# Where attention loads and w_out look-ahead stand in the bursts of a fused attention and two-MoE kernel

## The chip, the cores and the metric

The kernel runs on one core of one Trainium2 chip. The metric is device time in microseconds (us), the median of three runs. The engines are TensorE (PE), VectorE (DVE), ScalarE (ACT), GpSimd (POOL) and SyncE (SP). SP computes nothing here: it issues nearly all loads, in program order.

## What is computed

Attention in chunks of 64 tokens over 8 batches, 8 heads and 576 tokens, its output as 4608 rows of 512, and two gated products after it:

```python
attn = softmax(q_c @ k_c.T / 8)            # per chunk of 64, head dim 64
x = (attn @ v_c)                           # as 4608 x 512
x = ((x @ w_a) * (x @ w_b)) @ w_out        # 512 -> 1536 -> 512
h = ((x @ w1) * (x @ w2)) @ w3             # 512 -> 1024 -> 1024
out = h @ w_out2                           # 1024 -> 512
```

## The kernel before

The 4608 rows are nine blocks of 512. Phase 0 is the first gated product, phase 1 the second (w3 and its w_out are multiplied together once). In phase 0 the first pair of blocks is done by `plain_step`: 24 steps, in each the two products of one of 12 columns of 128 features, split in high and low parts (three matmuls for each product). The block written second lags by three steps (`order`, `AHEAD`). The next three pairs are done by `block_steps`, with a Strassen scheme of seven products (`strassen_step`); the ninth block stands alone.

Each pair leaves the second block's gated values in G tiles. They are multiplied with w_out only afterwards, in `burst`: 12 steps of 12 matmuls each in phase 0, one w_out tile of 128x1024 (512 KB) to a step. After its first step the burst also does the 12 matmuls that the pair before left pending. In parallel a list of pieces ("others") is worked off at one point per step, up to the eighth: DVE and ACT form the Strassen parts xP of the next pair. From the fifth step on the burst also advances attention for the pair after that. Phase 0 has four such bursts; below, the first stands ahead of the second pair, the second ahead of the third, the third ahead of the fourth pair.

Three queues of loads meet on SP in a burst:

- w_out tiles (`wo_f`), looked ahead by `Outs.ahead(n)`: it loads the next n tiles of the order into four homes. A home can be overwritten only when PE is done with the tile in it, so such a load can wait for PE, and all that follows on SP waits with it.
- attention loads (q and k of a unit as `qk`, v as `v`). A unit is one head pair of one block. They are put in a list by `ask` and issued one by one: `tick(loads=1)` at each of the four parts of a burst step, `tick(loads=3)` at each Strassen product; `settle(unit.qk_end)` issues all that are still due when a unit's `turn` is written. Units of the pair after the first use 32-wide rows, 16 transfers of 32 KB for q and k and ten for v.
- for the second pair only, parts of w_a and w_b: `first_sums[n].load()` (`su`, 512 KB) and `load_part` (`w_f_i`, 512 KB, or 256 KB for i = 3).

What moves on SP is thus set by where each call stands in the program and by the waits ahead of it; no planner is between. SP's transfers use eight semaphores in turn, so a transfer is issued only when the eighth before it has landed.

A `Track` emits its pieces in proportion to points that have passed, out of a number of points that is given to it. For the plain steps' attention that number was `4 * (len(order) - n) - 2`, here 82; steps with T = 1 call `point` three times and the others five, which makes 81 calls.

Of the kernel before, what the change touches and what calls it, by code (L numbers as in the profile page):

```python
# [78 lines left out]
def chunk_attention_two_gated_products(  # L79
# [59 lines left out]
    asks = {"left": deque(), "all": 0, "done": 0}  # L139
# [6 lines left out]
    def settle(n):  # L146
        while asks["done"] < n and asks["left"]:
            nc.sync.dma_start(*asks["left"].popleft())  # L148
            asks["done"] += 1

    def tick(every=False, loads=0):
        settle(asks["done"] + loads)
        for s in stores:
            s[0] += 1
        while stores and (every or stores[0][0] > 1):
            _, queue, to, src = stores.popleft()
            queue.dma_start(to, src)  # L157
# [92 lines left out]
    state = {"banks": ("rB", "rD")}  # L250
# [388 lines left out]
    def w_tile(n, name):  # L639
        return pool.tile([P, 2, 2, 2, P], F32R, tag=f"w{n}", name=name)  # L640

    def whole(t):
        return t.rearrange("p o s k n -> p (o s k n)")
# [94 lines left out]
    def load_part(ph, f, i):  # L738
        t = w_tile(4 * (f % 2) + i, f"w{ph}_{f}_{i}")
        if i < 3:  # L740
            nc.sync.dma_start(whole(t).bitcast(F32), dw[ph][f][0 if i == 0 else i + 1])
        else:
            nc.sync.dma_start(
                t[:, 0].rearrange("p s k n -> p (s k n)").bitcast(F32), dw[ph][f][1][:, NT:]
            )
        pairs.setdefault((ph, f), {})[i] = t
# [263 lines left out]
    def ready(ph, j, f, gplaces):  # L1010
        return g_parts(gplaces[f // 4][:, f % 4], f"{ph}_{j}b{f}", nc.gpsimd)

    def back(order):
        last = order[::-1]
        return [last[1], last[0], *last[2:]]

    def burst(ph, j, order, gplaces, others, at, first=None):

        n = NF[ph]
        order = back(order)  # L1020
        sums = []
        state["banks"] = ("acc2", "acc3")
        track = Track(others, 2 * n // 3)
        parts = [ready(ph, j, order[0], gplaces) if first is None else first]
        parts.append(ready(ph, j, order[1], gplaces))
        state["outs"].ahead(3)
        for f in range(n):
            if f and f + 2 < n:
                parts.append(ready(ph, j, order[f + 2], gplaces))
            s = Second(ph, j, f, state["outs"].next(), parts[f], sums, ("rC", "rA", "rB", "rD"))  # L1030
            s.part()
            s.part()
            track.point()
            if f > 3:
                for a in at:
                    a.point()
            s.rest()
            if f == 0:
                state["pending"].rest()
                parts.append(ready(ph, j, order[2], gplaces))  # L1040
            state["outs"].ahead(3)
        track.finish()
        state["pending"], state["banks"] = None_(), ("rB", "rD")

# [81 lines left out]
    with tc.manual_schedule():  # L1126
# [72 lines left out]
        order = plain_order(0, AHEAD)  # L1199
# [23 lines left out]
        units = unit_list(1)  # L1223
        both = attention_pieces(U[NHP:] + units)
        cut = 1 + 8 * NHP
        late = Track(both[:cut], 5 * AHEAD)
        at = None
        for n, (T, f) in enumerate(order):
            if T == 0:
                conv = Track([conv_piece()] * (1 if f == 0 else 3), 5 if f + 1 < AHEAD else 8)  # L1230
                if f + 1 == NF[0]:
                    conv = None
            if T == 1 and f == 0:
                late.finish()
                at = Track(both[cut:], 4 * (len(order) - n) - 2)

            def point(pe=True):
                if conv:
                    conv.point(pe)
                (at or late).point(pe)  # L1240

            if n + 1 == len(order):
                state["ready"] = ready(0, 1, NF[0] - 2, plain[0])
            plain_step(0, 0, T, f, f"0_{T}_{f}", point, plain[0], sums[0], "AC")
            if conv and (T == 1 or f + 1 < AHEAD):
                conv.finish()
                pump.flush()
# [106 lines left out]
        first_sums = {}  # L1354
        up = [list(range(n)) for n in NF]
        orders = {(0, 0): up[0]}
# [15 lines left out]
        for ph, sb in [(0, sb) for sb in range(1, NSB + 1)] + [(1, sb) for sb in range(NSB + 1)]:  # L1372
            lone = ph == 0 and sb == NSB
            begins = ph == 1 and sb == 0
            if begins:
                state["outs"] = Outs(1, wanted[1])
            state["outs"].ahead(2)
            if lone:
                x, pieces = lone_pieces(x32, f"{ph}{sb}")
                pieces = pieces + o2_pieces()  # L1380
                pump.cap = len(pump.jobs)
                pump.homes(["xo1", "xo2"], ["G2"])
                pieces += [(0.1, False, lambda: pump.load())] * 3
            elif not begins:
                x, pieces = strassen_pieces(x32, f"{ph}{sb}", sb == NSB)
            if ph == 0 and sb == 1:
                for n_ in range(2):
                    first_sums[n_] = summed(ph, orders[ph, sb][n_], n_)
                    first_sums[n_].load()
                for n_, i in ((0, 0), (0, 3), (1, 0)):  # L1390
                    load_part(ph, orders[ph, sb][n_], i)
                pieces = pieces + first_sums[0].pieces()
            steps, at, conv = NF[ph], [], []
            if ph == 0 and not lone:
                units = unit_list(sb + 1)
                attention_begins(units)
                if sb == 1:
                    settle(units[0].qk_end)
                    load_part(ph, orders[ph, sb][1], 3)
                work = attention_pieces(units)  # L1400
                n_pts = PTS * steps + steps - 4
                if sb == NSB - 1:
                    pump.cap += 3 * NF[1]
                    pump.homes(["Y0", "Y1"], ["Y2"])
                    for _ in range(3):
                        pump.load()
                    conv = later_conv(3 * NF[1])
                    work = merged((0, 1, work), (0, 1, conv))
                    n_pts = PTS * steps
                at.append(Track(work, n_pts - 3))  # L1410
            if not begins:
                done = (ph, sb - 1) if sb else (ph, 0)
                burst(ph, j + 1, orders[done], places, pieces, [] if conv else at, state.pop("ready", None))
            if lone:
                got = []
                for n_ in range(4):
                    load_w3(n_)
                at.append(Track(between(got), 5 * steps - 15))
                xs = {}

                def next_x():
                    diffs = deque()
                    for i in range(2):
                        t = pool.tile([P, 4, NT], F32, tag=f"G{i}", name=f"xd{i}")
                        diffs.extend(t[:, n_] for n_ in range(4))
                    xs["x"], xs["pieces"] = strassen_pieces(got, "10", diffs=diffs)

                early = [(0.1, False, lambda: (at[0].finish(), next_x()))]
                early += [(0.7, False, lambda n_=n_: xs["pieces"][n_][2]()) for n_ in range(18)]
                late = Track(early, 11)  # L1430
                class After:
                    n = 0

                    def point(self, pe=True):
                        self.n += 1
                        if self.n > 5 * steps - 15:
                            late.point(pe)

                    def finish(self):
                        late.finish()  # L1440

                at.append(After())
                lone_steps(ph, x, at)
                for p in xs["pieces"][18:]:
                    p[2]()
                x32, x = got, xs["x"]
                continue
            if ph == 1 and sb < NSB:
                got = []
                js = [LONE] if sb == NSB - 1 else [2 * sb + 2, 2 * sb + 3]  # L1450
                at.append(Track(x2_pieces(js, got), PTS * steps - 3))
            j, places = block_steps(ph, sb, x, at)
            if ph == 0:
                x32 = [u.x32 for u in units]
            elif sb < NSB:
                x32 = got
# [47 lines left out]
```

## Time and profile before

| | |
|---|---|
| median of three runs | 1638.82 us (1638.47 to 1640.89) |
| profiled execution | 1642.08 us, its span 1640.3 us |
| PE busy | 1559.8 us, 95% of the span |
| PEld / DVE / ACT / POOL busy | 76% / 52% / 34% / 30% |
| PE's share of the chain that ended last | 78% |
| DMA | 356.31 MB, mean 217 GB/s |

PE is busy almost throughout, so the time is PE's work plus the stretches in which PE waits or runs at a lower clock. Busy shares of the other engines say little; what matters is what ended each of PE's waits, and how SP's issues stand to it in time.

### The profile page before, as it was taken

How to read it: one execution, taken by the hardware profiler on the slowest of the kernel's cores; microseconds unless marked ns; L12 is line 12 of the kernel's file. 1: busy time of each engine (PE TensorE's matmuls, PEld its weight loads, DVE VectorE, ACT ScalarE, POOL GpSimd, SP SyncE). 2: the span in 40 equal slices, each digit the busy share in tenths (PEclk: the TensorE clock that was granted, in tenths of full speed). 3: DMA queues.
4: the chain of work that ended last, by engine and by line, in shares of the span. 5: the costliest groups of instructions: out<-in, count | busy, mean ns of one | idle time of the engine just before them, and what ended most of it. 6: DMA issues, size and time to landing. Idle time of an engine off the chain costs nothing.

```text
span 1640.3 us, 24184 instructions
## 1 busy us (share of the span) xinstructions
PE 1559.8 (95%) x8968; PEld 1254.6 (76%) x8968; DVE 858.3 (52%) x1384; ACT 551.4 (34%) x989; POOL 490.5 (30%) x502
## 2 busy tenths in 40 slices
PE   4889997899998999999999899999999999999998
PEld 3668776677777777787777677888878878878887
DVE  5667756486756555476775235545542442442331
ACT  5545444222343222433234223333421321321322
POOL 1223333222243211442225112223521421421422
PEclk8899998999999999999999999999999999999999
DMA  9977844787726787379984799776366266266184
GB/s 223 291 224 248 273 154 129 227 249 229 251 85 188 202 225 228 106 223 335 343 281 164 270 313 322 307 268 247 118 223 217 75 221 221 71 216 205 67 292 155
DMA packets 277013, 356.31 MB, mean 217 GB/s; under 512 B 174240, under 2 KB 194720, under 8 KB 276896
## 3 DMA queue, kind: packets, MB, share of 16 engines
q1 hardware_dynamic: 249728, 265.63, 52.9%
q0 software_dynamic: 23616, 81.80, 13.0%
q10 hardware_dynamic: 3552, 7.34, 1.3%
q8 instruction: 71, 1.16, 0.3%
q14 instruction: 46, 0.38, 0.1%
HBM read 268.70 MB, written 85.98 MB: 216 GB/s over the span
## 4 chain that ended last, share of the span: by engine, by line
PE 78%; DVE 6%; DMA 5%; issue 3%; ACT 3%; SPq 3%; POOL 1%; DVEq 0%; POOLq 0%; ACTq 0%
PE P L857 40%; PE acc L886 21%; PE pa L843 4%; PE pb L843 4%; PE wf L1115 3%; DMA wo<-dwo 3%; SPq L148 2%; PE pb0L L843 2%; PE pa0L L843 2%; PE x L407 1%; PE s L356 1%; DVE c L945 1%; DMA qk<-in_q_dram 1%; ACT xP L253 1%; PE t L478 1%
## 5 line engine op out<-in xcount | busy, mean ns | idle before, releaser
L857 PE MATMUL P<-xP,w 128*128 128x512 f32 (+1 forms) x3066 | 704.5, 382 | 11.6 <-DVE c L945 8.6
L857 PEld LDWEIGHTS P<-xP,w 128*128 128x128 f32 x3066 | 550.4, 188 | 135.2 <-DVE c L945 13.4
L945 DVE TENSOR_TENSOR c<-P,c 128x512 f32<-128x512 f32 (+1 forms) x228 | 150.4, 662 | 332.6 <-PE P L857 331.9
L942 ACT COPY c<-P 128x512 f32<-128x512 f32 (+1 forms) x228 | 128.4, 564 | 227.4 <-PE P L857 227.1
L973 POOL TENSOR_TENSOR G<-c,c 128x512 f32<-128x512 f32 x68 | 89.7, 1319 | 332.5 <-DVE c L945 332.4
L253 ACT CAST gh<-c 128x512 fp32r<-128x512 f32 x68 | 42.2, 621 | 329.6 <-DVE c L972 329.6
L254 POOL TENSOR_TENSOR gl<-c,gh 128x512 fp32r<-128x512 f32 x68 | 90.7, 1334 | 171.7 <-ACT gh L253 171.7
L886 PE MATMUL acc<-gh,wo 128*128 128x512 f32 x384 | 138.0, 397 | 0.0
L972 DVE TENSOR_TENSOR c<-P,c 128x512 f32<-128x512 f32 x68 | 47.0, 692 | 135.1 <-PE P L857 135.0
L886 PE MATMUL acc<-wo,gh 128*128 128x512 f32 x320 | 111.1, 390 | 0.5 <-ACT gh L253 0.5
L157 POOL DMA_DIRECT2D dw<-w x58 | 32.3, 558 | 176.5 <-DVE w L254 80.2
L886 PEld LDWEIGHTS acc<-gh,wo 128*128 128x128 f32 x384 | 72.5, 189 | 15.8
L254 DVE TENSOR_TENSOR xP<-xP,xP 128x512 fp32r<-128x512 f32 (+1 forms) x56 | 65.1, 1203 | 28.1 <-ACT xP L253 28.1
L843 PE MATMUL pa<-xq,w 128*128 128x512 f32 x288 | 76.0, 416 | 0.0
L886 PE MATMUL acc<-gl,wo 128*128 128x512 f32 x192 | 75.3, 392 | 0.0
L843 PE MATMUL pb<-xq,w 128*128 128x512 f32 x288 | 71.1, 396 | 0.0
L886 PEld LDWEIGHTS acc<-wo,gh 128*128 128x128 f32 x320 | 60.1, 188 | 13.4 <-ACT gh L253 1.0
L895 ACT COPY ev<-acc 128x512 f32<-128x512 f32 x72 | 42.4, 588 | 80.0 <-PE acc L886 75.1
L843 PEld LDWEIGHTS pa<-xq,w 128*128 128x128 f32 x288 | 57.0, 201 | 13.2 <-ACT xq L253 0.3
L886 PE MATMUL acc<-wo,gl 128*128 128x512 f32 x160 | 62.7, 392 | 0.8 <-POOL gl L254 0.8
L843 PEld LDWEIGHTS pb<-xq,w 128*128 128x128 f32 x288 | 52.9, 188 | 10.8
L373 ACT ACTIVATE e<-e 128x512 f32<-128x512 f32 x36 | 22.8, 632 | 90.5 <-DVE e L367 90.5
(158 smaller groups left out, 2369.8 us busy)
## 6 DMA issues: line engine op xcount, KB each, us to landing
w<-dw SPq DMA_DIRECT2D x175, 512.0 KB, 4.6
wo<-dwo SPq DMA_DIRECT2D x128, 512.0 KB, 4.5
dw<-w POOLq DMA_DIRECT2D x58, 512.0 KB, 4.2
w<-dw SPq DMA_DIRECT2D x75, 256.0 KB, 3.8
su<-d SPq DMA_DIRECT2D x20, 512.0 KB, 5.1
x2d<-ev POOLq DMA_DIRECT2D x36, 256.0 KB, 3.7
x<-x2d SPq DMA_DIRECT2D x36, 256.0 KB, 4.7
out_dram<-ev POOLq DMA_DIRECT2D x36, 256.0 KB, 3.0
```

Of the source, the lines that this page charges most:

```text
L148: nc.sync.dma_start(*asks["left"].popleft())
L253: nc.scalar.copy(dst_h, src)
L254: eng_l.tensor_tensor(dst_l, src, dst_h, op=ALU.subtract)
L843: nc.tensor.matmul(ps, w[m][:, kk // 2, wp, kk % 2], xq[kk // 2][:, kk % 2, xp], start=(n == 0), stop=(n == 3 * KM - 1),)
L857: nc.tensor.matmul(ps, w[:, wp, kt], x[:, kt, xp], start=(begins and n == 0), stop=(n == 5), skip_group_check=True,)
L886: nc.tensor.matmul(acc[m], a, b, start=(f == 0 and (wp, gp) == SEQ[0]), stop=(f == NF[ph] - 1 and (wp, gp) == SEQ[-1]),)
L895: nc.scalar.copy(t, acc[m])
L942: nc.scalar.copy(t, src)
L945: add = lambda o, a, b: nc.vector.tensor_tensor(o, a, b, op=ALU.add)
L972: nc.vector.tensor_tensor(g, last, c11, op=ALU.mult)
L973: nc.gpsimd.tensor_tensor(g_place(ph, nm.split("_")[0], f, gplaces), c22, c12, op=ALU.mult)
L1115: nc.tensor.matmul(ps, t[:, gp, jj], wo2[jj // 2][:, jj % 2, wp], start=(jj == 0 and (wp, gp) == SEQ[0]), stop=(jj == NF[1] - 1 and (wp, g ...
```

## The change

- In a burst, `state["hold"]` is set ahead of the first step and cleared after it. While it is set, `tick` issues no attention loads.
- After the first step `Outs.ahead` looks four tiles ahead in place of three, so the fifth tile's load is written one step earlier.
- For the second pair, two `su` loads and four `load_part` calls are no longer written ahead of the burst; they become six pieces among the others. The settling of the first unit's q and k ahead of the burst is gone.
- The number of points of the plain steps' attention track becomes the number of calls less three: 78 in place of 82.

```diff
     def tick(every=False, loads=0):
-        settle(asks["done"] + loads)
+        settle(asks["done"] + (0 if state.get("hold") else loads))
...
         track = Track(others, 2 * n // 3)
+        state["hold"] = True
...
             if f == 0:
                 state["pending"].rest()
                 parts.append(ready(ph, j, order[2], gplaces))
-            state["outs"].ahead(3)
+                state["hold"] = False
+            state["outs"].ahead(3 if f else 4)
...
-                at = Track(both[cut:], 4 * (len(order) - n) - 2)
+                at = Track(both[cut:], sum(3 if T_ else 5 for T_, _ in order[n:]) - 3)
...
             if ph == 0 and sb == 1:
+                begins_with = []
                 for n_ in range(2):
                     first_sums[n_] = summed(ph, orders[ph, sb][n_], n_)
-                    first_sums[n_].load()
-                for n_, i in ((0, 0), (0, 3), (1, 0)):
-                    load_part(ph, orders[ph, sb][n_], i)
+                    begins_with.append((0.1, False, first_sums[n_].load))
+                for n_, i in ((0, 0), (0, 3), (1, 0), (1, 3)):
+                    begins_with.append(
+                        (0.1, False, lambda f=orders[ph, sb][n_], i=i: load_part(ph, f, i))
+                    )
+                for n_, p in enumerate(begins_with):
+                    pieces.insert(4 + 3 * n_, p)
                 pieces = pieces + first_sums[0].pieces()
...
-                if sb == 1:
-                    settle(units[0].qk_end)
-                    load_part(ph, orders[ph, sb][1], 3)
```

On SP at the first burst, before: the six loads for the second pair and the first unit's q, k and v stand ahead of the burst's first w_out load, `wo_7` (the fifth tile that the burst uses).

```order
L763 DMA su_11_2887<-d_0_11_155 128x1024
L763 DMA su_10_2889<-d_0_10_154 128x1024
L741 DMA w_11_0_2891<-dw_11_0_108 128x1024
L743 DMA w_11_3_2893<-dw_11_1_109 128x512
L741 DMA w_10_0_2895<-dw_10_0_104 128x1024
L148 DMA qk_0_2897<-in_q_dram 32x8x32 x8
L148 DMA qk_0_2897<-in_k_dram 32x8x32 x8
L743 DMA w_10_3_2917<-dw_10_1_105 128x512
L148 DMA v_0_2898<-in_v_dram 64x2x64 x2
...
L148 DMA qk_1_2899<-in_q_dram 32x8x32 x2
L726 DMA wo_7_3011<-dwo_7_171 128x1024
```

On SP at the first burst, now, from the first w_out load on:

```order
L726 DMA wo_7_2947<-dwo_7_171 128x1024
L148 DMA qk_0_2887<-in_q_dram 32x8x32 x2
L763 DMA su_11_2961<-d_0_11_155 128x1024
L763 DMA su_10_2968<-d_0_10_154 128x1024
L148 DMA qk_0_2887<-in_q_dram 32x8x32 x4
L741 DMA w_11_0_2995<-dw_11_0_108 128x1024
L148 DMA qk_0_2887<-in_q_dram 32x8x32 x2
L726 DMA wo_6_3010<-dwo_6_170 128x1024
L148 DMA qk_0_2887<-in_k_dram 32x8x32 x2
L743 DMA w_11_3_3024<-dw_11_1_109 128x512
```

`wo_7` has moved ahead of all of them, and the six loads and the attention loads now stand between it and the later w_out tiles.

On SP at the end of the first burst, before, around `wo_0`, the tile of the burst's last step:

```order
L148 DMA v_1_2900<-in_v_dram 64x2x64 x4
L726 DMA wo_1_3220<-dwo_1_165 128x1024
L148 DMA qk_2_3125<-in_q_dram 32x8x32 x4
L726 DMA wo_0_3246<-dwo_0_164 128x1024
L148 DMA qk_2_3125<-in_q_dram 32x8x32 x4
```

And now:

```order
L148 DMA qk_1_2889<-in_q_dram 32x8x32 x4
L726 DMA wo_1_3198<-dwo_1_165 128x1024
L148 DMA qk_1_2889<-in_q_dram 32x8x32 x4
L148 DMA qk_1_2889<-in_k_dram 32x8x32 x8
L148 DMA v_1_2890<-in_v_dram 64x2x64 x2
L726 DMA wo_0_3234<-dwo_0_164 128x1024
```

Fourteen attention transfers stand between the last two tiles where four stood; twelve of them are settled for the second unit's `turn`.

On SP at the second burst, before (`wo_4` is again the fifth tile, `wo_11` the last):

```order
L148 DMA qk_0_4995<-in_q_dram 32x12x32 x4
L148 DMA qk_0_4995<-in_q_dram 32x4x32 x4
L148 DMA qk_0_4995<-in_k_dram 32x12x32 x4
L726 DMA wo_4_5088<-dwo_4_168 128x1024
...
L726 DMA wo_10_5288<-dwo_10_174 128x1024
L148 DMA qk_1_4997<-in_k_dram 32x12x32 x2
L148 DMA qk_1_4997<-in_k_dram 32x4x32 x4
L148 DMA v_1_4998<-in_v_dram 64x3x64 x2
L726 DMA wo_11_5318<-dwo_11_175 128x1024
```

And now:

```order
L726 DMA wo_4_5053<-dwo_4_168 128x1024
L148 DMA qk_0_4995<-in_q_dram 32x12x32 x4
L148 DMA qk_0_4995<-in_q_dram 32x4x32 x4
L726 DMA wo_5_5110<-dwo_5_169 128x1024
...
L726 DMA wo_10_5282<-dwo_10_174 128x1024
L148 DMA qk_1_4997<-in_q_dram 32x4x32 x4
L148 DMA qk_1_4997<-in_k_dram 32x12x32 x4
L148 DMA qk_1_4997<-in_k_dram 32x4x32 x4
L148 DMA v_1_4998<-in_v_dram 64x3x64 x2
L726 DMA wo_11_5318<-dwo_11_175 128x1024
```

Twelve q and k transfers moved from ahead of `wo_4` to behind it, and fourteen transfers stand ahead of `wo_11` where eight stood.

## Rows read from the trace of the kernel before

**Rows 1.** PE's waits over the span: releaser, us in total, times, longest

```profile
PE acc L886 <- DMA wo<-dwo: 15.2, 6, 7.4
```

**Rows 2.** Timeline of PE, first burst: start us, us, operation, count, [idle before, releaser]

```profile
261.57 0.50 PE L886 MATMUL acc<-gh_1b,wo 128*128 128x512 f32 x1
...
264.43 0.39 PE L886 MATMUL acc<-gh,wo 128*128 128x512 f32 x1
...
267.15 0.39 PE L886 MATMUL acc<-gh_1b,wo 128*128 128x512 f32 x1
...
283.18 0.76 PE L886 MATMUL acc<-gh_1b,wo 128*128 128x512 f32 x1 [7.40 <-DMA wo<-dwo]
...
308.35 0.51 PE L886 MATMUL acc<-gh_1b,wo 128*128 128x512 f32 x1 [2.65 <-DMA wo<-dwo]
...
312.76 7.03 PE L857 MATMUL P<-xP,w 128*128 128x512 f32 x30
```

**Rows 3.** Timeline of SP's issues in the first burst, same columns

```profile
260.28 4.71 SPq L148 DMA_DIRECT2D qk<-in_q_dram  x8
265.03 5.61 SPq L148 DMA_DIRECT2D qk<-in_k_dram  x8
...
271.18 6.45 SPq L148 DMA_DIRECT2D v<-in_v_dram  x10
...
278.92 0.34 SPq L726 DMA_DIRECT2D wo<-dwo  x1
279.31 1.91 SPq L148 DMA_DIRECT2D qk<-in_q_dram  x4
...
301.32 0.47 SPq L726 DMA_DIRECT2D wo<-dwo  x1
```

**Rows 4.** Windows: stretch, length, busy us of the engines, PEclk, DMA share, GB/s

```profile
275.00:280.00 5.00, 0.78 (x4) 0.32 (x2) 5.00 (x5) 1.36 (x3) 3.35 (x3) 0.79 0.24 47
280.00:285.00 5.00, 1.82 (x4) 1.49 (x5) 4.96 (x10) 1.22 (x2) 0.00 (x0) 0.50 0.92 248
...
470.00:480.00 10.00, 9.81 (x71) 7.76 (x70) 2.96 (x5) 1.82 (x4) 2.08 (x2) 1.00 0.01 2
...
500.00:520.00 20.00, 16.64 (x102) 13.18 (x101) 16.24 (x27) 5.04 (x9) 4.49 (x4) 1.00 0.65 168
```

**Rows 5.** Line 726's landing times, of its issues at 483.93, 508.74 and 301.32

```profile
DMA to landing us min/median/max: 3.4/3.4/3.4
...
DMA to landing us min/median/max: 4.8/4.8/4.8
...
DMA to landing us min/median/max: 6.9/6.9/6.9
```

**Rows 6.** Timeline of SP's issues ahead of and in the second burst

```profile
451.73 3.85 SPq L148 DMA_DIRECT2D qk<-in_q_dram  x8
455.63 1.97 SPq L148 DMA_DIRECT2D qk<-in_k_dram  x4
483.93 0.34 SPq L726 DMA_DIRECT2D wo<-dwo  x1
...
508.74 0.41 SPq L726 DMA_DIRECT2D wo<-dwo  x1
509.19 2.88 SPq L148 DMA_DIRECT2D qk<-in_k_dram  x6
...
514.23 0.54 SPq L726 DMA_DIRECT2D wo<-dwo  x1
```

**Rows 7.** Timeline of PE in the second burst: its two waits

```profile
503.68 0.69 PE L356 MATMUL s<-kT,qT 64*64 64x64 f32 x32 [1.81 <-DVE kT L345]
...
518.42 0.47 PE L886 MATMUL acc<-gh_3b,wo 128*128 128x512 f32 x1 [1.55 <-DMA wo<-dwo]
```

**Rows 8.** Timeline of SP in the third burst: its last six w_out issues

```profile
704.87 16.18 SPq L726 DMA_DIRECT2D wo<-dwo  x6
```

**Rows 9.** Timeline of PE, end of the plain steps

```profile
260.85 0.79 PE L407 MATMUL x<-pT,v 64*64 64x64 f32 x32 [1.01 <-ACT pT L494]
```

## The prediction

> **What bounds the kernel now.** I read the waits of PE first, since PE is busy for 95% of the span. Of what ends PE's waits, w_out tiles lead: 15.2 us in six waits [rows 1]. Two of these stand in the first burst and make up 10.05 us, 7.40 and 2.65 [rows 2]. The reader is to see there that 12 matmuls of one burst step take 2.72 us (264.43 to 267.15), and that the step behind the shorter wait, also 12 matmuls, takes 4.41 (308.35 to 312.76): 1.7 us more. The windows say why: the granted clock falls to 0.79 and then to 0.50 of full speed, that is to the lower of its two levels of 1.2 and 2.4 GHz, behind the long wait [rows 4]. So a wait costs its length and then up to another 2.7 us, if all 12 matmuls of a step take twice their 2.72.
>
> Next I read what SP did during the long wait. From 260.28 to 278.92 its track is a solid row of attention issues [rows 3], and the w_out tile that PE wants is issued only at 278.92, 4.3 us before PE goes on. While PE stood, the DMA engines were busy for 24% of 275 to 280 [rows 4]. The wait is thus one for SP's place in the queue, not for bandwidth. The numbers that I use of SP: a q or k transfer costs it 0.48 us when nothing presses (1.91 for four) and 0.65 in the busy start (16 from 260.28 to 270.64), a v transfer 0.645 (6.45 for ten), a contiguous one some 0.44 with its gap [rows 3]. A w_out tile lands 3.4 to 6.9 us after its issue [rows 5].
>
> **The change part by part. First burst.** PE would run it, never waiting, from 261.57 in a first step of 2.86, the pending 2.72, ten steps of 2.72 and 0.62 for the scores that stand inside (an estimate, the length of a 32-matmul attention group by the 0.69 in [rows 7]), and would want the last tile, `wo_0`, at about 295.0. `wo_7` can now be issued as soon as the first step is over, 264.4, and is there by 269 even at 4.8: the 7.40 us go, for that tile is wanted near 275.3. But SP still has to issue what lies between, and it starts on it only then: `wo_7` waits for PE, and all behind it waits too. From the order, between `wo_7` and `wo_0` stand 56 transfers: 32 of q and k, 12 of v, 12 contiguous ones (six for the second pair, six w_out tiles). At 0.57 for a q or k, the middle of its two prices: 32 x 0.57 = 18.2, 12 x 0.645 = 7.7, 12 x 0.44 = 5.3, `wo_7` itself 0.4. `wo_6` overwrites the tile of the third step, so it can't go before 272.6, where SP arrives at 271.0: 1.6. Sum 33.2, hence 297.9. No row shows six such loads inside a burst; they bring 2.5 MB, and each transfer waits until the eighth before it has landed. Eight issues at 0.48 take 3.8 us. Bounds: nothing, if the loads land in 3.4 us [rows 5], and 3 us, if three of the six land in 4.8 and hold SP for 1.0 each. I take 1.5, since DMA was already 92% busy in 280 to 285 with only two w_out tiles and attention in it [rows 4]. So `wo_0` goes out at 299.4 and lands, at 4.8, at 304.2. PE waits there for some 9 us, and the last step runs at the lower clock: with 4.4 to 5.4 us for it the burst ends near 309.1, against 312.76. **First burst: -3.7.** Its ends: q and k at 0.48, no hold-up, 3.4 to land, gives 304.2, or -8.6; q and k at 0.65, 3 us of hold-up and 6.9 to land gives 315.3, or +2.5.
>
> **Second burst.** Here the hold does harm. Before, the first twelve transfers of q and k were issued at 451.73 to 457.6 [rows 6], 26 us before `wo_4`, in a stretch that ends with the DMA engines nearly idle (1% of 470 to 480) [rows 4]. What hid them was the Strassen step that PE was in. Now `wo_4` stands ahead of them and waits for the burst's first step, so they are issued from 484.3 on. Eight of them fit in the gap in which SP waits for `wo_5` anyway; four more push later ones back, and by the order 14 transfers stand between `wo_10` and `wo_11` where eight stood. `wo_10` leaves at 508.74 as before, because it waits for PE. Then seven q and k by 512.6; the next must wait for `wo_10` to land, 508.74 + 4.8 = 513.5 [rows 5]; five more at 0.48 end at 516.0, two of v at 517.3. `wo_11` leaves 3.1 us after its 514.23. PE waited 1.55 for it [rows 7]; now 4.6. That lies between 2.65 and 7.40, and behind both the clock fell [rows 2], while behind 1.81 and 1.55 [rows 7] it stayed at 1.00 in 500 to 520 [rows 4]. So the last step costs another 1.7. **Second burst: +4.8.** Its ends: +1.4 (`wo_10` and `wo_11` land in 3.4, clock kept) and +6.8 (one us more of landing, 2.7 for the clock). The first unit's scores are not later for it: its last k goes out by 498 and has landed by 502, and PE got DVE's transpose only at 503.68 before, too [rows 7].
>
> The Trainium skill speaks against this part: "DMA: Bandwidth & Descriptors", section "Rules for kernel authors", says to issue a DMA early and to wait on it late, so that its fixed cost lies under compute. The rows of 451.73 to 457.6 agree, and by that rule alone the hold would only cost, here and in the first burst.
>
> **The rest.** In the third burst SP's last six w_out issues come 2.7 us apart, in the rhythm of PE's steps [rows 8]: SP waits for PE and not the other way. The hold puts twelve more transfers behind the first tile there too, some 6 us of issuing, most of which fits in such waits; the middle tiles then leave up to 0.5 us late. From the freeing of a home to the use of its next tile are two steps, 5.4 us, of which landing takes 3.4 to 4.8 [rows 5]: +0.3, with 0 and +1.5 as ends. In the fourth burst and in all four of phase 1 SP's order is word for word the same, because no attention is due and the fifth tile stands at the same place among SP's other rows: 0. The moved `su` and `w` loads are not missed where they were (they waited there for PE), and nobody needs them before the burst's last third. With 78 points in place of 82 attention's pieces in the plain steps come some 5% earlier. Its last unit's f and x still stand back to back, now one step earlier, so its 1.01 us of wait [rows 9] moves and stays; elsewhere short waits of that size may come or go: 0, with two of them (-2 and +2) as ends.
>
> **Sum:** -3.7 + 4.8 + 0.3 + 0 = +1.4. The profiled execution took 1642.08 us (span 1640.3), 3.3 more than the median; I know no reason for that to be in these bursts, so I add the sum to the median: 1638.82 + 1.4 = **1640.2**.
>
> **The rivals.** *Faster:* SP is less of a limit than I think. It issues at 0.48 all through, the six loads don't hold it up, `wo_0` is there by 299.6 (-8.6), and in the second burst the clock is kept (+1.4): -7.2, 1631.6. For it: the DMA engines had room in 275 to 280 [rows 4], and 1.91 for four [rows 3] is the price in the very burst. Against it: 16 transfers in a row took 0.65 each [rows 3], and just such runs of 16 and 12 now stand in the burst. *Slower:* in the first burst the wait for `wo_7` is exchanged for one as long for `wo_0`, since the second pair's 2.5 MB and 44 attention transfers have to pass ahead of it in a time in which PE needs only 30 us. With `wo_0` landing at 309.7 the burst ends at 315.3, +2.5, and the second burst's +4.8 stands: +7.3, 1646.1. It decides from `wo_0` landing after 306.4 on, since the burst then saves no more than 1.5. For it: the tile at 301.32 took 6.9 us to land [rows 5]. Against it: by my sum `wo_0` is issued two us before the 301.32 of before [rows 3], and other tiles landed in 3.4 to 4.8 [rows 5]. The skill's rule of the early issue leads to this case; the first burst of before speaks against it, where early issue was what made PE wait. *Without effect:* from the third burst on hardly any row of SP moves, so the change does nothing there; that is in the sum already.
>
> **How the numbers follow.** A measurement of this kernel can tell some 0.2% (3.3 us) from no change. My forecast, within 0.2%, gets 0.46; the faster rival 0.24; the slower one 0.30, more than the other because the second burst's loss rests on fewer assumptions than the first burst's gain. The likeliest's own range is 1635.5 to 1642.1. The ends of all terms together, -9.2 and +12.6, are not expected at once; the range for eight in ten runs from the faster rival to just past the slower: 1632 to 1647.
>
> **What would show it.** Right: in the first burst no wait of PE at the fifth step, a single one of 7 to 11 us at the last, SP solid from 264 to 300; in the second burst the first q and k behind 484, a wait of 4 to 5 us for `wo_11` and a slow step behind it; phase 1 as long as before. Wrong: `wo_0` there when PE wants it, so that the first burst is 10 us shorter; the second burst's clock at 1.00 throughout; or a difference that lies in the plain steps or behind the third burst.

## Result and profile after

The changed kernel takes 1649.79 us (median of five, 1647.92 to 1653.49) against 1638.82: a ratio of 1.0066, 95% interval 1.0048 to 1.0085. It is slower by 11 us, outside the range of 1632 to 1647. Its profiled execution took 1651.72 us, its span 1649.9.

To find where the time went I cut both traces at PE's first matmul of each stage and took the differences of the lengths. The third column is what the prediction had.

| stage | after less before, us | predicted |
|---|---|---|
| start, up to the first product | +0.5 | 0 |
| plain steps, up to the first burst's first matmul | +2.4 | 0 |
| first burst (51.19 to 51.07) | -0.1 | -3.7 |
| Strassen steps of the second pair | +1.6 | 0 |
| second burst (40.3 to 45.4) | +5.1 | +4.8 |
| Strassen steps of the third pair | +0.1 | 0 |
| third burst (36.0 to 38.4) | +2.4 | +0.3 |
| Strassen steps of the fourth pair | -0.2 | 0 |
| fourth burst | -2.0 | 0 |
| all that follows | -0.1 | 0 |
| sum | +9.7 | +1.4 |

The -2.0 of the fourth burst is no gain of the change: of the six kernels below that are as before from the second burst on, four are shorter there by 2.0 to 2.1 us and two longer by 0.8 to 1.0. A single profiled execution carries such chances; the difference of the medians is 11.0. The execution of before that was profiled is one of them: it took 3.3 us more than its median, and for all thirteen kernels below the stages add up to less than the difference of the medians, by 0.7 to 5.9 us. In which stage that execution was long is not settled; what p_points says of it stands there.

PE's waits after the change, over the span, in the columns of [rows 1] (waiting line, releaser: us in total, times, longest):

```profile
PE acc L886 <- DMA wo<-dwo: 18.6, 8, 6.4
```

The waits for w_out did not shrink from the 15.2 us of [rows 1]; they grew to 18.6.

**First burst.** PE's timeline after the change, to hold against [rows 2] (start us, us, operation, count, [idle before, releaser]):

```profile
264.47 0.50 PE L886 MATMUL acc<-gh_1b,wo 128*128 128x512 f32 x1 [0.85 <-DVE G0p L996]
...
282.04 0.47 PE L886 MATMUL acc<-gh_1b,wo 128*128 128x512 f32 x1 [0.65 <-DMA wo<-dwo]
...
287.15 0.47 PE L886 MATMUL acc<-gh_1b,wo 128*128 128x512 f32 x1 [2.13 <-DMA wo<-dwo]
...
310.31 0.76 PE L886 MATMUL acc<-gh_1b,wo 128*128 128x512 f32 x1 [6.37 <-DMA wo<-dwo]
...
315.54 0.64 PE L857 MATMUL P<-xP,w 128*128 128x512 f32 x2
```

The 7.40 us at the fifth step are gone, as meant. In their place stand 0.65, 2.13 and 6.37, and the last step takes 5.23 us (310.31 to 315.54) in place of 2.72. SP's timeline shows why `wo_0` is late (to hold against [rows 3]):

```profile
267.55 0.35 SPq L726 DMA_DIRECT2D wo<-dwo  x1
267.95 2.50 SPq L148 DMA_DIRECT2D qk<-in_q_dram  x2
270.61 0.87 SPq L763 DMA_DIRECT2D su<-d  x2
...
277.61 0.34 SPq L726 DMA_DIRECT2D wo<-dwo  x1
...
295.83 0.39 SPq L726 DMA_DIRECT2D wo<-dwo  x1
296.57 1.79 SPq L148 DMA_DIRECT2D qk<-in_q_dram  x4
298.40 6.44 SPq L148 DMA_DIRECT2D qk<-in_k_dram  x8
304.89 1.26 SPq L148 DMA_DIRECT2D v<-in_v_dram  x2
306.25 0.54 SPq L726 DMA_DIRECT2D wo<-dwo  x1
```

`wo_7` goes out at 267.55, one step after the burst's start, and `wo_0` at 306.25: 38.7 us for what stands between. The last 10.4 of these (295.83 to 306.25) go to 14 attention transfers, 12 of them settled at one place for the second unit's `turn`; eight k alone take 6.44. What SP waited for between the two issues (268 to 306.3), in the columns of [rows 1]:

```profile
SPq L148 <- DMA w<-dw: 1.8, 3, 1.3
SPq L726 <- DMA su<-d: 1.6, 1, 1.6
...
SPq L726 <- PE s L356: 0.6, 1, 0.6
```

With two smaller rows for w_out tiles (0.7 and 0.3) this is 4.4 us until an earlier transfer had landed, and with one more for PE (0.3) only 0.9 us for PE.

The windows (stretch, length, busy us of PE, PEld, DVE, ACT, POOL, granted clock, DMA share, GB/s), to hold against [rows 4]:

```profile
275.00:280.00 5.00, 5.00 (x24) 4.13 (x23) 5.00 (x4) 4.25 (x8) 4.48 (x4) 1.00 1.09 341
280.00:285.00 5.00, 4.35 (x19) 2.99 (x17) 5.00 (x8) 1.75 (x3) 1.39 (x2) 1.00 1.07 342
...
310.00:315.00 5.00, 4.69 (x11) 3.75 (x12) 1.86 (x4) 1.65 (x3) 1.12 (x2) 0.50 0.47 128
```

The DMA engines, 24% busy in 275 to 280 before, are now full from 275 to 285. After its wait PE runs at the lower clock (0.50) in 310 to 315.

**Second burst.** SP and then PE after the change, to hold against [rows 6] and [rows 7]:

```profile
488.30 0.32 SPq L726 DMA_DIRECT2D wo<-dwo  x1
488.71 3.94 SPq L148 DMA_DIRECT2D qk<-in_q_dram  x8
...
513.72 0.41 SPq L726 DMA_DIRECT2D wo<-dwo  x1
514.17 1.85 SPq L148 DMA_DIRECT2D qk<-in_q_dram  x4
516.07 3.91 SPq L148 DMA_DIRECT2D qk<-in_k_dram  x8
520.02 1.30 SPq L148 DMA_DIRECT2D v<-in_v_dram  x2
521.42 0.54 SPq L726 DMA_DIRECT2D wo<-dwo  x1
```

```profile
525.71 0.76 PE L886 MATMUL acc<-gh_3b,wo 128*128 128x512 f32 x1 [4.50 <-DMA wo<-dwo]
```

The first q and k are issued behind `wo_4`, at 488.71, 14 transfers stand between `wo_10` and `wo_11`, and PE waits 4.50 us. Its last step then runs at a granted clock of 0.50 (525 to 530).

**Third burst.** PE after the change; before, it never waited for w_out there:

```profile
717.39 0.47 PE L886 MATMUL acc<-gh_5b,wo 128*128 128x512 f32 x1 [1.09 <-DMA wo<-dwo]
724.01 0.47 PE L886 MATMUL acc<-gh_5b,wo 128*128 128x512 f32 x1 [0.54 <-DMA wo<-dwo]
```

**Plain steps.** PE's waits in 100 to 265, of before and then of after:

```profile
PE x L407 <- ACT pT L494: 1.6, 2, 1.0
PE f L491 <- DVE e L381: 1.3, 2, 0.6
PE s L356 <- ACT x L421: 0.5, 1, 0.5
```

```profile
PE t L478 <- issue: 3.4, 2, 1.7
PE x L407 <- ACT pT L494: 1.1, 3, 0.7
PE acc L886 <- DVE G0p L996: 0.9, 1, 0.9
```

3.4 us of waits became 5.4. Two of the new ones, 1.69 each, stand ahead of a unit's transposes on PE (L478), where "issue" names nothing that the profile shows; the 0.85 stands ahead of the burst's first matmul, which now waits for DVE's gated values.

**Strassen steps of the second pair.** The same wait of 1.82 us for DVE, in before and in after:

```profile
380.53 1.66 PE L857 MATMUL P<-xP,w 128*128 128x512 f32 x6 [1.82 <-DVE c L945]
```

```profile
383.37 2.62 PE L857 MATMUL P<-xP,w 128*128 128x512 f32 x6 [1.82 <-DVE c L945]
```

Behind it six matmuls take 1.66 us in the one and 2.62 in the other, because the granted clock fell to 0.78 in 385 to 390.

### The profile page after: what moved, and what is told of

Its sections match the earlier page's. It is cut to its first block, busy times and chain, and to the rows that moved or that the text cites. A ratio compares the mean times of both kernels' runs of the same rounds, so it can differ in the third digit from the quotient of the medians.

```text
span 1649.9 us, 24177 instructions
## 1 busy us (share of the span) xinstructions
PE 1564.0 (95%) x8968; PEld 1255.4 (76%) x8968; DVE 855.8 (52%) x1384; ACT 550.8 (33%) x989; POOL 491.2 (30%) x502
## 4 chain that ended last, share of the span: by engine, by line
PE 79%; DVE 6%; DMA 5%; issue 3%; SPq 3%; ACT 3%; POOL 1%; DVEq 0%; POOLq 0%; ACTq 0%
PE P L857 40%; PE acc L886 21%; PE pa L843 4%; PE pb L843 4%; PE wf L1117 3%; SPq L148 2%; PE pb0L L843 2%; PE pa0L L843 2%; DMA wo<-dwo 2%; PE x L407 1%; PE s L356 1%; DMA w<-dw 1%; DVE c L945 1%; DMA qk<-in_q_dram 1%; DMA qk<-in_k_dram 1%
## 5 line engine op out<-in xcount | busy, mean ns | idle before, releaser
L945 DVE TENSOR_TENSOR c<-P,c 128x512 f32<-128x512 f32 (+1 forms) x228 | 150.5, 662 | 335.1 <-PE P L857 334.4
L843 PEld LDWEIGHTS pa<-xq,w 128*128 128x128 f32 x288 | 56.3, 200 | 12.8
```

The source lines that it names most:

```text
L843: nc.tensor.matmul(ps, w[m][:, kk // 2, wp, kk % 2], xq[kk // 2][:, kk % 2, xp], start=(n == 0), stop=(n == 3 * KM - 1),)
L945: add = lambda o, a, b: nc.vector.tensor_tensor(o, a, b, op=ALU.add)
```

## Experiments

The theory after the result: in the first burst each of the two edits (the hold with its early tile, and the moved six loads) takes `wo_7`'s wait away by itself. Together they leave no attention load and no weight load ahead of the burst, so all goes through SP behind `wo_7`, and the wait comes back at the last tile. The hold costs something in the second and third burst as predicted; the points cost two of PE's waits in the plain steps. The rivals: the six loads fill the DMA engines and are alone to blame; the differences outside the bursts are chances of one execution. Each run is compared with before on its own chip, where before took 1637.6 to 1639.7.

The stages of all runs, each less before in us, and the times with their ratio to before on the same chip:

| kernel | plain | burst 1 | Strassen 2 | burst 2 | burst 3 | median us, ratio (95%) |
|---|---|---|---|---|---|---|
| p_points | +2.5 | -4.1 | +1.6 | -0.5 | -0.2 | 1642.97, 1.0035 (1.0019 to 1.0052) |
| p_hold | +1.7 | -9.6 | -0.1 | +5.1 | +1.4 | 1638.83, 1.0002 (0.9988 to 1.0017) |
| hold_only | 0.0 | -9.6 | 0.0 | +5.2 | +2.2 | 1637.68, 0.9997 (0.9985 to 1.0008) |
| p_hold_first | +1.3 | -9.6 | +1.6 | +0.7 | -0.3 | 1634.63, 0.9975 (0.9957 to 0.9994) |
| hold_first_4all | +1.3 | -8.3 | +2.4 | -0.3 | -0.2 | 1635.28, 0.9976 (0.9958 to 0.9993) |
| p_loads | +1.1 | -7.3 | +3.3 | -0.4 | -0.4 | 1636.45, 0.9988 (0.9975 to 1.0001) |
| quiet_first | -1.5 | -13.1 | +37.1 | +1.2 | +0.4 | 1661.23, 1.0142 (1.0123 to 1.0161) |
| changed kernel | +2.4 | -0.1 | +1.6 | +5.1 | +2.4 | 1649.79, 1.0066 (1.0048 to 1.0085) |
| a_no_points | -0.4 | -0.6 | +1.1 | +5.0 | +2.4 | 1649.62, 1.0061 (1.0037 to 1.0086) |
| a_first_only | +4.0 | -0.1 | +2.7 | +0.6 | -0.3 | 1645.73, 1.0039 (1.0024 to 1.0053) |
| a_loads_early | +3.7 | +0.3 | +1.2 | +5.2 | +2.9 | 1653.87, 1.0086 (1.0060 to 1.0111) |
| a_qk_early | +1.1 | -4.9 | +1.6 | +5.1 | +1.8 | 1644.66, 1.0024 (1.0005 to 1.0042) |
| a_ahead4_all | +3.8 | -7.1 | +11.1 | +3.4 | +1.9 | 1654.73, 1.0095 (1.0065 to 1.0125) |

The plain column holds about +-1.5 us of chance: kernels whose plain steps are those of before, word for word, lie between -1.5 and +1.7, since the granted clock of 40 to 140, 0.85 to 1.00, and short waits there differ from one execution to the next.

### One part of the change alone

The points alone:

```diff
-                at = Track(both[cut:], 4 * (len(order) - n) - 2)
+                at = Track(both[cut:], sum(3 if T_ else 5 for T_, _ in order[n:]) - 3)
```

> The kernel before with one edit: 78 points for the plain steps' attention in place of 82. Theory: of the 10 us lost, 2.4 lie in the plain steps and come from this edit (other neighbours of attention's transposes, and G0p waited for at the burst's start); expected +2 to +3 us, 1641 to 1642, with the first burst starting 2 to 3 us later. Rival: the 2.4 us were chance of one execution (clock, waits that the profile calls issue); expected 0, within 1 us of before.

The trace shows the waits of the changed kernel at the same places. PE's timeline:

```profile
144.31 1.06 PE L478 MATMUL t<-ident,qk 128*128 128x128 f32 x8 [1.69 <-issue]
```

All six kernels here with 78 points have two waits of 1.68 or 1.69 at L478, and none of those with 82 has them. So the points cost 2.0 us of waits. In this kernel's profiled execution the first burst gives the time back: its two waits for w_out are 7.02 and 1.46 in place of 7.40 and 2.65 [rows 2], and its last step keeps the full clock and takes 2.8 us in place of 4.4.

The median rose by 5.2 us, more than the 2 to 3 expected and than the stages, which add up to 0.0. Without the burst's -4.1 they would add up to 4.1. The burst's steps and SP's order in it are those of before; whether its 47.1 us in place of 51.2 are a chance of one execution or come with the 78 points is not shown. The column "burst 1" is held against the 51.2 of that one execution. If they were a chance of it, all entries of the column are some 4 us too low, the -0.1 of the changed kernel too; the differences among the other kernels don't rest on it.

The hold and the early fourth tile in all bursts (p_hold), and the hold with three tiles ahead everywhere (hold_only):

```diff
+        state["hold"] = True
...
+                state["hold"] = False
-            state["outs"].ahead(3)
+            state["outs"].ahead(3 if f else 4)
```

> The kernel before with the hold and the four-tile look-ahead only; the second pair's loads stay ahead of the burst. Theory (place in SP's queue): in the first burst wo_7 goes out near 271.5 and is there in time, 32 small transfers stand between it and wo_0, which lands near 298; that burst ends some 10 us earlier; the second burst loses 5 us as in the changed kernel. Sum -5, about 1634. Rival: the hold itself harms the first burst too, because loads that lay under the plain steps come late; then no gain there and +5 in all, 1644.

> The kernel before with the hold in all bursts, but three tiles ahead everywhere. Theory (the hold alone pushes the first twelve q and k behind: 14 transfers between wo_10 and wo_11 as in the changed kernel): second burst 45 to 46 us (40.3 before), a wait of 4 to 5 us for wo_11 and the lower clock behind it; third burst +1.5 to +3; first burst 42 to 45 us, a little longer than with the early fourth tile (41.6); in all 1638 to 1641. Rival (the tile that is looked ahead, for which SP waits, does it): second and third burst within 1 us of before, 1632 to 1635.

Both first bursts are 9.6 us shorter, so the early tile brings nothing; the hold alone does it. Both second bursts lose 5.1 to 5.2, by a wait for w_out of 4.28 and 4.51. PE in hold_only:

```profile
511.94 0.77 PE L886 MATMUL acc<-gh_3b,wo 128*128 128x512 f32 x1 [4.51 <-DMA wo<-dwo]
```

The rival for hold_only (the looked-ahead tile does it) falls. The times tell little: gain and losses nearly cancel, -2 to -3 by the three bursts, and the interval of hold_only runs from -2.5 to +1.3 us. The 1634 expected of p_hold was not reached.

Why the hold gains so much by itself is in p_hold's SP timeline:

```profile
261.88 4.78 SPq L148 DMA_DIRECT2D qk<-in_q_dram  x8
266.71 4.89 SPq L148 DMA_DIRECT2D qk<-in_k_dram  x8
...
272.31 0.34 SPq L726 DMA_DIRECT2D wo<-dwo  x1
272.70 5.63 SPq L148 DMA_DIRECT2D v<-in_v_dram  x8
```

The first unit's q and k are still settled ahead of the burst and go out while PE is at the burst's first steps; only v and the second unit's moved behind `wo_7`, which leaves at 272.31 in place of 278.92 [rows 3], and the fifth step waits 0.43.

The six loads moved into the burst, with no hold and no settling:

```diff
-                    first_sums[n_].load()
+                    begins_with.append((0.1, False, first_sums[n_].load))
...
-                if sb == 1:
-                    settle(units[0].qk_end)
-                    load_part(ph, orders[ph, sb][1], 3)
```

> The kernel before with only the second pair's six loads moved among the burst's pieces (and the settling of the first unit ahead of the burst gone); no hold, three tiles of look-ahead, 82 points. Theory (place in SP's queue): w_11_0 no longer waits for PE ahead of everything, so ten q and k transfers go out before the burst; wo_7 leaves near 264.5, wo_0 near 291.5, and the first burst runs with 1 us of waits: -13 us, about 1626. The second burst is as before. Rival (bandwidth: it is the six loads' 2.5 MB inside the burst that keep wo_0 late): the burst gains less than 5 us, 1634 or more.

Here, too, `wo_7` is early (265.72), and the first burst gains 7.3, between the theory's 13 and the rival's 5. SP's timeline:

```profile
233.03 4.62 SPq L148 DMA_DIRECT2D qk<-in_q_dram  x8
...
265.72 0.34 SPq L726 DMA_DIRECT2D wo<-dwo  x1
```

Without the six loads ahead of them, all q and k of the first unit but four k transfers were out before 241, though nothing settled them: by the program the `tick` calls of the burst's first two steps and of the pending matmuls between, four each, issued them. In the changed kernel the hold stops eight of these calls and the early fourth tile goes ahead of the others, and its first q and k leave at 267.95. Some of the gain is lost in the Strassen steps (+3.3, waits for DVE's adds). So each part alone takes most of the 10 us of [rows 2], and both together take nothing by this trace: -0.1.

### Which loads make the last tile late

The six loads ahead of the burst again, all else as changed:

```diff
-                for n_, p in enumerate(begins_with):
-                    pieces.insert(4 + 3 * n_, p)
+                for p in begins_with:
+                    p[2]()
```

> The changed kernel with the six w_a and w_b loads written ahead of the first burst again (the settling of the first unit's q and k stays away). Theory A (the six loads fill the DMA engines in 270 to 285 and hold SP's queue up): without them in the burst the DMA share stays under 0.95 there, wo_0 leaves at 296 to 299 in place of 306.25, the wait of 6.4 us at the last step is at most 3.5, the burst 43 to 46 us in place of 51.1: 5 to 8 us less than the changed kernel's 1649.8, 1642 to 1645. Theory B (the 44 attention transfers that stand behind wo_7 are enough): wo_0 leaves after 303, the burst is longer than 49 us, 1648 to 1650.

Theory A fell; the burst is what theory B expected, and the time lies above its 1650. SP and PE of this kernel:

```profile
300.05 6.42 SPq L148 DMA_DIRECT2D qk<-in_k_dram  x8
...
307.87 0.54 SPq L726 DMA_DIRECT2D wo<-dwo  x1
```

```profile
289.95 1.13 PE L356 MATMUL s<-kT,qT 64*64 64x64 f32 x32 [3.53 <-DVE kT L345]
...
311.93 0.77 PE L886 MATMUL acc<-gh_1b,wo 128*128 128x512 f32 x1 [6.08 <-DMA wo<-dwo]
```

Without the six loads the DMA share in 275 to 280 is 0.55, but the burst is no shorter. `wo_0` leaves 42.5 us after the burst's start, where it was 41.8 in the changed kernel. What remains is the rhythm of PE (the tiles before `wo_0` wait for it, and it waits 3.53 for the first unit's transposes) and then the same settling of twelve q and k. SP's only waits in 268.8 to 307.9:

```profile
SPq L726 <- PE acc L886: 8.1, 4, 4.3
```

In place of 4.4 us for landings in the changed kernel, SP now stands 8.1 us for PE. The six loads had merely filled SP's pauses.

The first unit's q and k settled ahead of the burst again, the six loads inside:

```diff
+                if sb == 1:
+                    settle(units[0].qk_end)
                 work = attention_pieces(units)
```

> The changed kernel with the first unit's 16 q and k transfers settled ahead of the first burst again; the six loads stay inside the burst. Theory (what fills SP's queue behind wo_7 is those 16 transfers, which lost the cover of the plain steps): between wo_7 and wo_0 stand 16 q and k in place of 32, some 9 us less; wo_0 leaves before 299, the wait at the last step is at most 3 us, the burst 42 to 45 us in place of 51.1, the whole 6 to 9 us less than the changed kernel: 1641 to 1644. Rival (hold and six loads inside the burst can't go together whatever else stands there): burst over 49 us, 1648 to 1650.

The burst shortens by 4.8 us against the changed kernel, to 46.3; the q and k are out by 235, and `wo_0` leaves at 299.10. PE:

```profile
287.47 0.47 PE L886 MATMUL acc<-gh_1b,wo 128*128 128x512 f32 x1 [4.22 <-DMA wo<-dwo]
...
306.09 0.47 PE L886 MATMUL acc<-gh_1b,wo 128*128 128x512 f32 x1 [2.42 <-DMA wo<-dwo]
```

The theory had the end right (wait at the last step 2.42, expected at most 3) and the middle wrong: the seventh step waits 4.22 for `wo_5`, issued at 280.17 behind two of the six loads, with the DMA engines 97% busy in 280 to 285. The time, 1644.66, and the burst of 46.3 us both lie just above what was expected. So the six loads do cost, by their landing times, once q and k are out of the way. With p_hold this makes a square, first burst less before (p_hold has 82 points, the others 78; in the changed kernel 82 make its burst 0.5 us shorter):

| | six loads ahead | six loads inside |
|---|---|---|
| first unit's q and k settled ahead | -9.6 | -4.9 |
| not settled ahead | +0.3 | -0.1 |

Settling those 16 small transfers ahead of `wo_7` is worth 9.9 us with the loads ahead and 4.8 with them inside. Moving the loads inside costs 4.7 where the 16 are settled ahead, and nothing where they are not.

Four tiles ahead after every step of the first burst, so that `wo_0` stands ahead of the second unit's twelve q and k:

```diff
-            state["outs"].ahead(3 if f else 4)
+            state["outs"].ahead(3 if f and (ph or j != 1) else 4)
```

> The changed kernel with four tiles ahead after every step of the first burst in place of the first alone, so that wo_0 stands ahead of the second unit's 12 q and k (SP needed 9.7 us for the 14 transfers between wo_1 and wo_0). Theory (that settling is what makes wo_0 late): wo_0 leaves some 9 us earlier, the wait of 6.4 us and the lower clock behind it go, the burst is 43 to 46 us long in place of 51.1, 1642 to 1645. Rival (the queue is simply too full, the lateness goes to the second unit's q and k): the burst shortens but PE waits for the second unit's scores, burst and Strassen step together within 2 us of the changed kernel: 1648 to 1650.

The wait at the last step went, as the theory had it, but the rival is right about the sum, and it is worse than that. PE:

```profile
292.21 0.90 PE L356 MATMUL s<-kT,qT 64*64 64x64 f32 x32 [4.89 <-DVE kT L345]
...
429.03 2.91 PE L857 MATMUL P<-xP,w 128*128 128x512 f32 x6 [3.23 <-DVE c L945]
```

PE waits for DVE instead. Against before, the burst gains 7 us and the Strassen steps lose 11. By these waits the attention that comes late to DVE makes its adds for PE (L945) late as well.

No attention in the first burst at all, its loads held to the burst's end:

```diff
-        settle(asks["done"] + loads)
+        settle(asks["done"] + (0 if state.get("hold") else loads))
...
-                    settle(units[0].qk_end)
...
-                burst(ph, j + 1, orders[done], places, pieces, [] if conv else at, state.pop("ready", None))
+                burst(ph, j + 1, orders[done], places, pieces, [] if conv or quiet else at, state.pop("ready", None))
```

> The kernel before with no attention loads and no attention pieces in the first burst at all (they start in the Strassen steps behind it); the six loads stay ahead of the burst. Theory: SP then carries only w_out tiles, no wait for them is left (10 us) and the clock stays up (4 us): -14 in the burst; attention for eight units in 12 steps without the burst's eight points costs 0 to 3 us there; -11 to -14, about 1626. Rival (bandwidth or DVE is the burst's limit): less than 5 us gained.

The burst runs without a wait for w_out and is 13.1 us shorter, which is at most the price of all that stands in SP's way there, since attention's matmuls left the burst as well. The bill comes in the Strassen steps, +37, where 0 to 3 was expected. PE:

```profile
313.42 1.13 PE L356 MATMUL s<-kT,qT 64*64 64x64 f32 x32 [9.74 <-DVE c L945]
329.84 11.43 PE L857 MATMUL P<-xP,w 128*128 128x512 f32 x36 [10.25 <-DVE c L945]
```

### Only the first burst, and without the points

The hold and the early tile in the first burst alone, on the kernel before (p_hold_first) and on the changed one (a_first_only):

```diff
+        state["hold"] = ph == 0 and j == 1
...
+            state["outs"].ahead(3 if f or j != 1 or ph else 4)
```

> The kernel before with the hold and the four-tile look-ahead in the first burst alone. Theory (the later bursts lose because their first q and k lay under the Strassen step ahead of them): first burst 41.6 us long as with the hold everywhere (51.2 before), second and third burst as before (40.3 and 36.0), no wait of 4 to 5 us for wo_11; 6.5 us less than the 1638.8 of the hold everywhere, 1632 +-2. Rival (the second and third burst's extra time is a chance of that execution, not the hold): 1638 to 1639, no different from the hold everywhere.

> The changed kernel with the hold and the four-tile look-ahead in the first burst alone. Theory: second burst -5.1, third -2.4, the rest as in the changed kernel: 1642.3 +-2. Rival (these two are chances of one execution): 1648 to 1650.

In both the second and third burst are back within 0.7 us of before. p_hold_first is, with hold_first_4all below, the best kernel here, 0.25% below before (0.06% to 0.43%); its wait for `wo_11` is 0.69.

a_first_only came out 3.4 us above what was expected: the bursts gave back 7.2, but its plain steps and Strassen steps were 2.7 longer than those of the changed kernel.

Four tiles ahead at each step of that first burst as well:

```diff
+            state["outs"].ahead(3 if ph or j != 1 else 4)
```

> The kernel before with the hold in the first burst alone and four tiles ahead after each of its steps. Theory: the waits for w_out that the hold with one early tile left in the first burst (0.43, 1.28 and 0.57 us) go, nothing takes their place: burst 39 to 40.5 us in place of 41.6, 1632 to 1634 where the hold in the first burst alone took 1634.6. Rival (SP now waits for PE at each tile and the attention loads behind it come later): PE waits over 1.5 us more for DVE's transposes, 1635 to 1638.

The waits for w_out went and one of 3.31 for DVE's transposes came: the rival's exchange. The time is that of p_hold_first.

The changed kernel with 82 points:

```diff
-                at = Track(both[cut:], sum(3 if T_ else 5 for T_, _ in order[n:]) - 3)
+                at = Track(both[cut:], 4 * (len(order) - n) - 2)
```

> The changed kernel with 82 points in the plain steps, as before. Theory A (the 2.4 us of the plain steps and the 0.85 at the burst's start come from the points alone): plain steps as before, 1.01 in place of 0.85 at the end, 2.4 us less, 1647.4; with the lower clock near 380, which both kernels with 78 points showed, gone too: 1645.8. Theory B (the points cost what 78 alone cost when timed, 5 us): 1644 to 1645. Theory C (nothing): 1649 to 1650.

In the trace the two waits of 1.69 are gone and the plain steps are 2.8 us shorter; in the time nothing is seen (theory C), with an interval of some 4 us on each side, while p_points alone showed 5.2. So the times don't agree on the points, and the 2.0 us rest on the trace alone.

## Why the prediction was wrong, point by point

What failed is the sizes of terms: SP's time from `wo_7` to `wo_0` in the first burst (34.7 us counted, 38.7 measured), the third burst (+0.3 counted, +2.4 measured) and the two terms put at 0, the plain steps (+2.4) and the second pair's Strassen steps (+1.6). The second burst held.

- **First burst, -3.7 predicted, -0.1 measured.** The mechanism was right (the wait for `wo_7` goes, one for `wo_0` takes its place, the last step runs at the lower clock). Between `wo_7` and `wo_0` I counted 33.2 us and 1.5 of hold-up; it took 38.7. Of the 4.0 us by which `wo_0` is later against the burst's start (41.8 in place of 37.8), 1.9 lie in the last 14 transfers: 10.4 where 8.5 were counted, because the eight k cost 0.8 each on average, not 0.57. The other 2.1 had been lost before, most of it in waits until earlier transfers had landed: 4.4 us, where I had 1.5 for this and 1.6 for a wait for PE, which fell away. PE's own waits of 0.65 and 2.13, which I had not counted, follow from the tiles that left late. The forecast's -3.7 and these 4.0, less the 0.7 by which PE went on sooner after `wo_0`'s issue (4.1 us in place of 4.8), and 0.3 for a last step of 5.23 in place of 4.9, make -0.1.
- **The time to start from.** I added the sum to the median because I knew no reason for the 3.3 us of the profiled execution to lie in these bursts. p_points, with 47.1 us in the same first burst, may be one; with that burst as the start the change would cost some 4 us there. It is not settled.
- **The six loads.** I gave them 1.5 us of hold-up on SP, and 4.4 were measured. But a_loads_early shows that nothing is gained by taking them away alone. Their cost and that of the late q and k hide behind each other.
- **What I did not ask.** The 32 q and k transfers were counted one by one, and that count was right, but I didn't ask which of them had had a cover before. The 16 of the first unit had stood ahead of `wo_7`; they lost that place by the hold with its early tile and the end of their settling together (p_loads, without the hold, had 12 of them out before 241). By the square this alone, with no load moved, uses up the hold's 9.6 us; the moved loads alone use up 4.7. The Trainium skill ("DMA: Bandwidth & Descriptors", section "Rules for kernel authors") says to issue early and wait late; I had weighed it against the first burst of before and put it down as contradicted. The square above agrees with it: those 16 issued early are worth 4.8 to 9.9 us.
- **Second burst, +4.8 predicted, +5.1 measured.** Right in the mechanism: first q and k at 488.7, 14 transfers, a wait of 4.50 (4.6 predicted) and the lower clock behind it. hold_only shows that it is the hold. One step in it did not come: SP did not stand until `wo_10` had landed, and the 12 q and k behind it ran on at 0.48 each; `wo_11` left 2.8 us later against the burst's start, not 3.1, part of that because `wo_10` itself was 0.6 late. Here some luck is in the number.
- **Third burst, +0.3 predicted, +2.4 measured,** 1.4 to 2.9 in all seven runs that hold there. The step that failed: I let most of the twelve transfers fit into SP's waits, so that tiles leave up to 0.5 us late and land in at most 4.8. The eighth tile did leave 0.4 late against the burst's start (711.65; 701.63 before), but took 5.6 us to land, and the tenth left 2.9 late (719.28; 706.77 before). PE waits 1.09 and 0.54 for them; the other 0.7 us I can't name.
- **Plain steps, 0 predicted with -2 and +2 as ends, 2.0 by the waits.** I took "moves and stays" from one wait [rows 9] and didn't follow the other units' transposes, ahead of which the two waits of 1.69 came.
- **Strassen steps, 0 predicted, +1.6.** Not foreseen, and not settled (below).
- **The rivals.** The one on the slow side, 1646.1, came nearest: `wo_0` landed at 310.3, that is 307.4 on the forecast's scale, whose burst starts at 261.6, later than its point of 306.4. But its first burst, +2.5, was not measured either (-0.1), so part of its nearness is luck; the terms that it left out (plain steps, third burst, Strassen steps: 6.4 together) carry the time past it to 1649.8.
- **Its arithmetic.** 264.4 and 33.2 make 297.6, not 297.9, and the upper ends add up to +12.8, not +12.6; neither changes the forecast by more than 0.3 us.

## What to carry to other kernels

When loads share one in-order queue, ask of every load that is moved what covered it before, and add up what stands between the next two loads that someone waits for; two edits that each remove the same wait can take each other's cover away. A hold in such a queue is paid wherever the held loads had lain under other work, so put it only where the trace shows a wait that it ends. After a wait of several us (4.50 and 6.37 here) look for the lower clock as a second payment, stage by stage.

## What the runs showed of the hardware

- The price of one small transfer on SP is not fixed: 32 KB q and k cost 0.49 us each where eight went out alone (3.94 at 488.71) and 0.80 on average in the settling at 298.40 (6.44 for eight; most still took some 0.49, the longest 1.83).
- A w_out tile of 512 KB was there 3.9 us after its issue at 306.25 (DMA share 0.49 in 305 to 310), and 7.2 us after the one at 280.17 in a_qk_early, with a share of 0.97 in 280 to 285.
- The clock behind one and the same wait of 1.82 us in the second pair's Strassen steps: six matmuls took 1.66 us in eight of the traces and 1.82 to 2.81 in five. All five have 78 points; of the six kernels with 78 points only a_loads_early kept the clock, and those with 82 that have this wait all did. Why it falls in the one group is open; it was not tried further.
